# A tuned attention and two-layer MoE kernel: the second layer's sort in two parts, fifteen tiles in the first layer's slot 17 and twelve at the seam

## The chip, the core and the metric

The kernel runs on one core of one Trainium2 chip. A core has five engines with queues of their own: TensorE (PE in the rows; PEld is its weight load), VectorE (DVE), ScalarE (ACT), GpSimd (POOL) and SyncE (SP, which here issues most DMA transfers). Each engine takes its instructions in the order in which the program gives them to it; between engines semaphores hold an instruction back until what it needs is there. The metric is device microseconds (us) for one execution.

## The reference, cut to what matters

Attention over 4 batches of 576 tokens makes x of 2304 rows and 512 columns (not touched here). Two mixture-of-experts layers follow, each with eight experts and one expert for each token:

```python
def _moe2_ref(x, modality_id, w_gate, modality_bias, w1, w2) -> np.ndarray:
    ...
    logits = x @ w_gate + modality_bias[modality_id]
    e_idx = np.argmax(logits, axis=1)
    ...
    gate_w = probs[np.arange(N), e_idx]
    ...
    for e in range(E):
        mask = e_idx == e
        ...
        h = np.maximum(x[mask] @ w1[e], 0.0)
        out[mask] = gate_w[mask, None] * (h @ w2[e])
```

`probs` is the softmax of the logits. The first layer is the same but for a second gate in place of the modality's bias.

## The kernel before, in words

**Slots.** A layer (`moe`, L789 on) works through slots. A slot is one tile of up to 128 tokens that go to the same expert, padded where an expert's last tile isn't full. Slots 0 to 17 always run; slots 18 to 26 stand in nested `tc.If` blocks and run while the number of slots, found at run time, is larger. In slot `s`, `slot()` issues 96 matmuls `ph<-xT,wb` (L834) in two halves of 48, `mm1(0)` and `mm1(1)`; after each half ScalarE makes `hh` (L844) and VectorE `hl` (L845); then 24 matmuls `py<-wb,hh` and `py<-wb,hl` (L905) make the result, 16 with hh and 8 with hl. The two first slots of a layer take their tokens from `xsA` and go to the expert that most tokens want (`first_expert`, `first_slots`, made during the end of the stage before, from part of the tokens); their result stays in `pya0` and `pya1` until the gates are known.

**Weights.** When the expert changes, SP loads 4 MB of f32 weights into `raw` in eight pieces (L89), and ScalarE and VectorE split them into high and low f16 halves `wb` (L97, L102). In slots `s` from 3 on this is done piece by piece inside branches that ask at run time whether the slot after next needs it (`part`, L859). The second layer's slots 0 to 2 use one expert whose weights were loaded and split during the first layer (`Fill`); slot 3 (`KE`) always turns to new weights, and which expert these are stands in the table `tab`.

**Results of the first layer.** In slot `s`, `post.out(s - 1)` takes the previous slot's result out of PSUM: ScalarE writes its high half (L1036), VectorE its low half (L1037). `post.turn(s - 1)` lets TensorE transpose the row of halves behind `mm1(1)` (L1055, eight transposes, the first four on the high half, the last four on the low half), VectorE copies that into `yT` (L1056), TensorE makes the second layer's logits from it (`router`, L1064) and VectorE adds them into `lg2` (L1073). In slot 17 the router runs twice, so that `lg2` is complete up to tile 16 at its end.

**The sort.** `sort()` (L609) is a generator. Between its `yield`s stand the steps that turn logits into slots. Step one classifies: VectorE takes the maximum over eight experts (L620), finds which expert it is (L623 to L632) and counts along the tiles (L635). Step two is TensorE's rank matmuls `ct` and `rk` (L639 to L642). Step three makes positions: VectorE from `cmp` (L646) to the slot and row of each token, `pi` (L675), and the slot matrix `ob` (L679), from which GpSimd makes `obt` (L680) and ScalarE `obp` (L681). Step four lays out rows: `A` is a matrix of 128 columns for each tile with a one in the token's row, made in pieces of nine tiles (L686). Step five is the index matmuls `pidx`, two for each tile (L691, L692). Step six writes `idx` (L696) and issues three gathers of rows from `y_dram` on GpSimd (L797). Step seven, the table, is a chain of VectorE operations from L704 to L732 that ends in `tab`; then TensorE turns slot 2's gathered rows (L812), and SP loads slot 3's weights and transposes its rows. Step eight makes the gates, step nine sums them (`pg`, L772, L774).

**What sets the order.** Nothing is scheduled automatically. `at(s, k, f)` hangs a function at hook `k` of slot `s`: hook 0 is at the slot's start, 8 behind the first eight matmuls, 1 and 4 inside the first and second half (two thirds through), 2 behind the first half and ahead of its hh and hl, 3 behind them, 5 behind the second half's hh and hl and the previous row's transposes, 6 behind 12 of the 24 `py` matmuls, 7 at the slot's end. Before the change the second layer's sort hung wholly in the second layer:

```python
at(0, 8, lambda: post1.router(None), run(so2))
at(0, 6, run(so2))
at(0, 7, run(so2, 2))
at(1, 6, run(so2, 2))
at(1, 7, run(so2))
at(2, 0, run(so2))
```

The seam is the stretch from the first layer's last slot to the second layer's slot 3. With this input the first layer runs 23 slots: slot 17 lies at about 365 to 378 us of the trace, slot 18 starts at 378.23, and the second layer's slot 0 starts its matmuls at 437.42.

## Time and profile before

| | |
|---|---|
| median of 3 runs | 660.2 us (659.15 to 666.1) |
| the profiled execution, its own time | 661.31 us |
| its span in the trace | 659.5 us, mean granted clock 0.953 |
| busy: PE, PEld, DVE, ACT, POOL | 591.5, 459.4, 358.2, 268.9, 204.9 us |

All times in rows are microseconds from the span's start. A row of the timeline has the start, the length of the merged group, the engine, the line, the operation with output and input, how many were merged (x96) and, in brackets, how long the engine had been idle before and what it was released by. A row of the view by stretch has the stretch, its length, the busy time of PE, PEld, DVE, ACT and POOL with the number of instructions in brackets, then TensorE's granted clock as a share of full speed, the busy share of the DMA engines and GB/s. Releasers are inferred: where the engine named had long been done, it was something else, often a DMA.

### The profile page before, as it was taken

What the parts mean: (1) busy time and instruction counts of PE and PEld (TensorE: products, weight loads), DVE (VectorE), ACT (ScalarE), POOL (GpSimd) and SP (SyncE); (2) the same over time, 40 slices, a digit from 0 to 9 for tenths busy, and PEclk for the clock granted to TensorE, in tenths of its full rate; (3) what the DMA queues carried; (4) which work ended last, traced back from release to release, by engine and by line L of the source; (5) the groups of instructions that cost most, each with busy time, mean ns of one, the idle gap of its engine ahead of it and who ended that gap; (6) DMA issues with size and microseconds to landing.
All of it is one profiled execution on the core that took longest, in us unless ns stands there. A gap on an engine that the chain in (4) does not pass through costs nothing. (4 is left out here: it accounts for less than half of the span.)

```text
span 659.5 us, 19565 instructions
## 1 busy us (share of the span) xinstructions
PE 591.5 (90%) x7440; PEld 459.4 (70%) x7440; DVE 358.2 (54%) x656; ACT 268.9 (41%) x398; POOL 204.9 (31%) x327
## 2 busy tenths in 40 slices
PE   3889978942998999999999999989889999999994
PEld 2778877842786776868687686866667767676772
DVE  4699987867848625963848922248351010113560
ACT  4678766642245324833627511111242111123450
POOL 2467677615351111101102410002463312121220
PEclk9789999975798999999999999989899999999997
DMA  9999999997399964995878871500995434243921
GB/s 205 230 233 229 243 223 249 254 271 211 86 330 317 341 162 104 345 321 136 232 222 213 228 141 49 59 28 2 238 357 144 106 89 84 65 97 83 309 57 42
DMA packets 108514, 120.99 MB, mean 183 GB/s; under 512 B 72047, under 2 KB 76911, under 8 KB 107376
## 3 DMA queue, kind: packets, MB, share of 16 engines
q1 hardware_dynamic: 102720, 101.71, 61.7%
q0 software_dynamic: 5280, 17.13, 8.4%
q8 instruction: 60, 0.98, 0.7%
q10 hardware_dynamic: 400, 0.72, 0.5%
q14 instruction: 54, 0.44, 0.2%
HBM read 214.11 MB, written 18.22 MB: 352 GB/s over the span
## 5 line engine op out<-in xcount | busy, mean ns | idle before, releaser
L834 PEld LDWEIGHTS <-wb 128*128 128x128 f16 x4032 | 234.2, 100 | 10.3 <-issue 5.1
L834 PE MATMUL ph<-xT,wb 128*128 128x128 f16 x3648 | 213.5, 221 | 2.8 <-ACT y L1036 1.1
L845 DVE SCALAR_TENSOR_TENSOR hl<-ph,hh 128x512 f16<-128x512 f32 x84 | 57.8, 689 | 169.5 <-ACTq L859 152.0
L905 PE MATMUL py<-wb,hh 128*128 128x512 f16 x608 | 137.6, 379 | 1.6 <-ACTq L859 1.6
L905 PEld LDWEIGHTS <-hh 128*128 128x128 f16 x672 | 63.8, 98 | 70.4 <-ACTq L859 1.7
L102 DVE SCALAR_TENSOR_TENSOR wb<-raw,wb 128x1024 f16<-128x1024 f32 (+1 forms) x80 | 102.9, 1326 | 18.1 <-ACT wb L97 17.9
L844 ACT ACTIVATE hh<-ph 128x512 f16<-128x512 f32 x84 | 50.1, 597 | 147.5 <-PE ph L834 147.0
L97 ACT ACTIVATE wb<-raw 128x1024 f16<-128x1024 f32 (+1 forms) x80 | 86.9, 1133 | 12.0 <-ACTq L859 3.1
L905 PE MATMUL py<-wb,hl 128*128 128x512 f16 x304 | 71.9, 379 | 0.0
L905 PEld LDWEIGHTS <-hl 128*128 128x128 f16 x336 | 32.8, 98 | 39.9 <-DVE hl L845 0.4
L1160 POOL DMA_INDIRECT out<-y,idx x16 | 16.2, 1010 | 97.9 <-ACTq L859 77.7
L421 PE MATMUL po<-v,pT 128*96 128x65 f32 x384 | 39.3, 253 | 1.2 <-DMA v<-in_vw 1.2
L421 PEld LDWEIGHTS po<-v,pT 128*96 128x96 f32 x384 | 36.1, 169 | 1.6 <-DMA v<-in_vw 1.5
L797 POOL DMA_INDIRECT xg<-x_dram,idxaa x23 | 26.7, 1161 | 28.1 <-DMA xT<-xg 17.3
L407 PE MATMUL pst<-mt,msel 128*128 128x96 bf16 x192 | 30.6, 219 | 2.3 <-ACT mt L395 2.2
L362 DVE TENSOR_REDUCE M<-ps 96x4 f32<-96x512 f32 x48 | 31.5, 679 | 2.0 <-PE ps L361 1.9
L1159 ACT ACTIVATE y<-py,gsb 128x512 f32<-128x512 f32 x16 | 11.0, 686 | 52.3 <-PE py L905 52.3
L319 DVE SCALAR_TENSOR_TENSOR kl<-qk,kh 128x608 f16<-128x608 f32 x32 | 28.5, 892 | 7.0 <-ACT kh L316 7.0
L360 PEld LDWEIGHTS <-qs 128*96 128x96 f16 x192 | 24.5, 132 | 11.2 <-DVE qs L341 6.2
L360 PE MATMUL ps<-kh,qs 128*96 128x128 f16 x192 | 29.5, 232 | 2.8 <-ACT kh L316 2.8
L410 ACT ACTIVATE pT<-pst 128x384 f32<-128x384 f32 x48 | 23.4, 488 | 19.3 <-PE pst L409 18.7
L361 PE MATMUL ps<-kl,qs 128*96 128x128 f16 x192 | 29.3, 232 | 1.8 <-DVE kl L319 1.8
(401 smaller groups left out, 750.2 us busy)
## 6 DMA issues: line engine op xcount, KB each, us to landing
raw<-in_w1a SPq DMA_DIRECT2D x95, 512.0 KB
raw<-in_w2a SPq DMA_DIRECT2D x92, 512.0 KB
raw<-in_w1b SPq DMA_DIRECT2D x75, 512.0 KB
raw<-in_w2b SPq DMA_DIRECT2D x72, 512.0 KB
qk<-in_qk SPq DMA_DIRECT2D x16, 608.0 KB
v<-in_vw SPq DMA_DIRECT2D x16, 390.0 KB
qk<-in_qk SPq DMA_DIRECT2D x16, 304.0 KB
y_dram<-y SPq DMA_DIRECT2D x11, 260.0 KB
```

The costliest lines, as they stand in the source:

```text
L97: nc.scalar.activation(wb[:, 0, s], raw[:, s], AF.Copy, scale=SW)
L102: nc.vector.scalar_tensor_tensor(out=wb[:, 1, s], in0=raw[:, s], scalar=SW, in1=wb[:, 0, s], op0=ALU.mult, op1=ALU.subtract)
L319: nc.vector.scalar_tensor_tensor(out=kls[n][:, h], in0=krs[n][:, h], scalar=SQK, in1=khs[n][:, h], op0=ALU.mult, op1=ALU.subtract)
L360: nc.tensor.matmul(ps[:, j, :], st, kh[:, h, QT * i:QT * i + 128], start=False, stop=False, skip_group_check=True)
L361: nc.tensor.matmul(ps[:, j, :], st, kl[:, h, QT * i:QT * i + 128], start=False, stop=j == 3, skip_group_check=True)
L362: nc.vector.tensor_reduce(out=Ms[n][:, 4 * g:4 * g + 4], in_=ps, axis=AX.X, op=ALU.max)
L407: nc.tensor.matmul(ps[:, j, :], msel[:, typ, j, :], mt[:, g, :], start=j == 0, stop=False, skip_group_check=True)
L421: nc.tensor.matmul(po[:, i, :], pT[:, NQ * h + i, :], v[:, h, i, :], start=True, stop=True)
L834: nc.tensor.matmul(ph[:, j, :], w[:, c, fs], xT[:, parts[c + i], :], start=k == 0, stop=k == 47, skip_group_check=True)
L844: nc.scalar.activation(hs, ph, AF.Relu)
L845: nc.vector.scalar_tensor_tensor(out=hl[:, 4 * g:4 * g + 4, :], in0=ph, scalar=0.0, in1=hs, op0=ALU.max, op1=ALU.subtract)
L905: nc.tensor.matmul(to, a, w, start=k == 0, stop=k == len(ops) - 1)
```

## The change

The sort of the second layer becomes two parts. The first fifteen of its 27 tiles (`PRE`) are classified at hook 5 of the first layer's slot 17, ranked among themselves, and given their rows within their expert and the part of `A` for them at hook 7 of that slot; these numbers don't depend on how many blocks each expert gets, only the slot does. At the seam only twelve tiles are classified and ranked, the first part's counts being added by one more matmul to `ct` and one to `rk`; positions are made for all tiles, `A` for the last twelve. The hooks at the seam move too: the rank matmuls from hook 6 of slot 0 to hook 4, the index matmuls and gathers from hook 6 of slot 1 to hook 2, the table from hook 7 to 6, the gates from hook 0 of slot 2 to hook 7 of slot 1, the gates' sums and the first splits of new weights to earlier hooks of slot 2. `oh` and `inc` are now laid out part by part.

```diff
+PRE = 15
...
-    for n in (NT, NSLOT):
+    for n in (NT, PRE, NSLOT - PRE):
...
+        def classify(a, b):
+            n = b - a
+            sh = [P, n, E]
+            v.tensor_reduce(out=mx[:, a:b], in_=lg[:, a:b], axis=AX.X, op=ALU.max)
+            v.tensor_tensor(eq[:, a:b], lg[:, a:b], mx[:, a:b].unsqueeze(2).to_broadcast(sh), op=ALU.is_equal)
+            v.tensor_tensor(eq[:, a:b], eq[:, a:b], desc.unsqueeze(1).to_broadcast(sh), op=ALU.mult)
+            v.tensor_reduce(out=mi[:, a:b], in_=eq[:, a:b], axis=AX.X, op=ALU.max)
+            if inv is not None:
+                v.scalar_tensor_tensor(out=mi[:, a:b], in0=inv[:, a:b], scalar=16.0, in1=mi[:, a:b], op0=ALU.mult, op1=ALU.add)
+            c = min(max(ca, a), b)
+            own = mi
+            if a < c:
+                own = mb
+                v.scalar_tensor_tensor(out=mb[:, a:c], in0=ea["cons"][:, a:c], scalar=16.0, in1=mi[:, a:c], op0=ALU.mult, op1=ALU.add)
+                if c < b:
+                    v.tensor_copy(mb[:, c:b], mi[:, c:b])
+            v.tensor_tensor(part(ohs, a, b).rearrange("p e t -> p t e"), eq[:, a:b], own[:, a:b].unsqueeze(2).to_broadcast(sh), op=ALU.is_equal)
+            v.tensor_tensor_scan(incs[:, E * a:E * b], masks[n].rearrange("p e t -> p (e t)"), ohs[:, E * a:E * b], 0.0, op0=ALU.mult, op1=ALU.add)
+
+        def ranks(a, b):
+            rk = pp.tile([P, E, b - a], F32, name="rk", tag="pw")
+            nc.tensor.matmul(rk, lt1, part(ohs, a, b), start=True, stop=False)
+            nc.tensor.matmul(rk, ones, part(incs, a, b), start=False, stop=a == 0)
+            if a:
+                nc.tensor.matmul(rk, ones, part(incs, 0, a)[:, :, a - 1:a].to_broadcast([P, E, b - a]), start=False, stop=True)
+            return rk
+
+        def rows(a, b):
+            for a in range(a, b, ACH):
+                n = min(ACH, b - a)
+                v.tensor_tensor(A[:, a:a + n], iota_row.unsqueeze(1).to_broadcast([P, n, P]),
+                                pi[:, 2, a:a + n].unsqueeze(2).to_broadcast([P, n, P]), op=ALU.is_equal)
+
+        ps_ = T("ps", [E, -1])
+        if pre:
+            classify(0, pre)
+            yield
+            rk = ranks(0, pre)
+            yield
+            within = T("within", [-1])
+            v.tensor_tensor(ps_[:, :, :pre], rk, part(ohs, 0, pre), op=ALU.mult)
+            v.tensor_reduce(out=within[:, :pre], in_=ps_[:, :, :pre].rearrange("p e t -> p t e"), axis=AX.X, op=ALU.add)
+            v.tensor_tensor(within[:, :ca], within[:, :ca], ea["consr"], op=ALU.add)
+            v.tensor_copy(pi[:, 0, :pre], within[:, :pre])
+            v.tensor_scalar(pi[:, 2, :pre], pi[:, 0, :pre], 127, None, op0=ALU.bitwise_and)
+            yield
+            rows(0, pre)
+            yield
+        classify(pre, nt)
         yield
...
+        nc.tensor.matmul(ct, ones, part(incs, pre, nt)[:, :, nt - pre - 1], start=True, stop=not pre)
+        if pre:
+            nc.tensor.matmul(ct, ones, part(incs, 0, pre)[:, :, pre - 1], start=False, stop=True)
+        rk = ranks(pre, nt)
...
-        ps_ = T("ps", [E, -1])
-        v.scalar_tensor_tensor(out=ps_, in0=rk, scalar=float(KA * P), in1=base.unsqueeze(2).to_broadcast([P, E, nt]), op0=ALU.add, op1=ALU.add)
-        v.tensor_tensor(ps_, ps_, oh, op=ALU.mult)
+        if pre:
+            v.scalar_tensor_tensor(out=ps_[:, :, :pre], in0=base.unsqueeze(2).to_broadcast([P, E, pre]), scalar=float(KA * P), in1=part(ohs, 0, pre), op0=ALU.add, op1=ALU.mult)
+        v.scalar_tensor_tensor(out=ps_[:, :, pre:], in0=rk, scalar=float(KA * P), in1=base.unsqueeze(2).to_broadcast([P, E, nt - pre]), op0=ALU.add, op1=ALU.add)
+        v.tensor_tensor(ps_[:, :, pre:], ps_[:, :, pre:], part(ohs, pre, nt), op=ALU.mult)
         pos = T("pos", [-1])
         v.tensor_reduce(out=pos, in_=ps_.rearrange("p e t -> p t e"), axis=AX.X, op=ALU.add)
-        v.tensor_tensor(pos[:, :ca], pos[:, :ca], ea["consr"], op=ALU.add)
-        pi = T("pi", [3, -1], I32)
+        if pre:
+            v.tensor_tensor(pos[:, :pre], pos[:, :pre], within[:, :pre], op=ALU.add)
+        else:
+            v.tensor_tensor(pos[:, :ca], pos[:, :ca], ea["consr"], op=ALU.add)
         if inv is None:
             v.tensor_copy(pi[:, 0], pos)
         else:
             v.scalar_tensor_tensor(out=pi[:, 0], in0=inv, scalar=8192.0, in1=pos, op0=ALU.mult, op1=ALU.add)
         v.tensor_scalar(pi[:, 1], pi[:, 0], 7, None, op0=ALU.logical_shift_right)
-        v.tensor_scalar(pi[:, 2], pi[:, 0], 127, None, op0=ALU.bitwise_and)
+        v.tensor_scalar(pi[:, 2, pre:], pi[:, 0, pre:], 127, None, op0=ALU.bitwise_and)
...
-        A = T("A", [-1, P], F16)
-        for a in range(0, nt, ACH):
-            n = min(ACH, nt - a)
-            v.tensor_tensor(A[:, a:a + n], iota_row.unsqueeze(1).to_broadcast([P, n, P]),
-                            pi[:, 2, a:a + n].unsqueeze(2).to_broadcast([P, n, P]), op=ALU.is_equal)
+        rows(pre, nt)
...
+    def sort2(n=1):
+        def go():
+            if not sorts:
+                sorts.append(sort("b", lg2, NSLOT, start1.inv, fe2, early[1], tabs[1], 1.0, None, [], 1 / (SX2 * SW * SW), start2, PRE))
+            for _ in range(n):
+                next(sorts[0], None)
+        return go
+
+    for s, k in ((15, 0), (15, 7), (16, 0), (16, 3), (16, 5), (16, 7), (17, 0), (17, 7)):
+        at(s, k, slots2)
+    at(17, 5, sort2())
+    at(17, 7, sort2(3))
+    py1 = moe(w1a, w2a, tabs[0], x_dram, (0, 1, 4, 5, 2, 3, 6, 7), post1, start1, wbuf)
...
-    at(0, 8, lambda: post1.router(None), run(so2))
-    at(0, 6, run(so2))
-    at(0, 7, run(so2, 2))
-    at(1, 6, run(so2, 2))
-    at(1, 7, run(so2))
-    at(2, 0, run(so2))
-    at(2, 5, lambda: start2.first_splits(FIRST[0]), lambda: start2.first_splits(FIRST[1]))
-    at(2, 6, run(so2), lambda: start2.first_splits(FIRST[2]), lambda: start2.first_splits(FIRST[3]))
+    at(0, 8, lambda: post1.router(None), sort2())
+    at(0, 4, sort2())
+    at(0, 7, sort2(2))
+    at(1, 2, sort2(2))
+    at(1, 6, sort2())
+    at(1, 7, sort2())
+    at(2, 3, lambda: start2.first_splits(FIRST[0]))
+    at(2, 5, sort2(), *(lambda i=i: start2.first_splits(FIRST[i]) for i in (1, 2)))
+    at(2, 6, lambda: start2.first_splits(FIRST[3]))
```

**Place 1, VectorE from slot 17's last hl to slot 18's first operation.** The rows are VectorE's instructions in program order. `hl` is the second half's low part, `yT` the copy of the transposed row, `wb` the weight splits in their branches, `lg` the logits of tile 16, `lotmp` the low half of slot 17's result. Before:

```order
L845 SCALAR_TENSOR_TENSOR hl<-ph_6832,hh 128x512
L1056 COPY yT_2814<-pyt 128x1024
L859 COMPARE_AND_BRANCH
L102 SCALAR_TENSOR_TENSOR wb_69<-raw,wb_69 128x1024 x3
L859 UNCONDITIONAL_BRANCH x2
L855 TENSOR_LOAD tab_2800
L859 COMPARE_AND_BRANCH
L102 SCALAR_TENSOR_TENSOR wb_2779<-raw,wb_2779 128x1024 x3
L859 UNCONDITIONAL_BRANCH x2
L1073 SCALAR_TENSOR_TENSOR lg_78<-plg,lg_78 128x8
L922 COMPARE_AND_BRANCH
L1037 SCALAR_TENSOR_TENSOR lotmp<-py,gsa,lotmp 128x512
```

And now, first behind the copy of yT (hook 5):

```order
L1096 COPY yT_2817<-pyt 128x1024
L632 TENSOR_REDUCE mxb<-lg_78 128x15
L633 TENSOR_TENSOR eqb<-lg_78,mxb 128x120
L634 TENSOR_TENSOR eqb<-eqb,cft 128x120
L635 TENSOR_REDUCE mib<-eqb 128x15
L637 SCALAR_TENSOR_TENSOR mib<-inva,mib 128x15
L642 SCALAR_TENSOR_TENSOR mbb<-ea_cons_85,mib 128x13
L644 COPY mbb<-mib 128x2
L645 TENSOR_TENSOR ohb<-eqb,mbb 128x15x8
L646 SCALAR_TENSOR_TENSOR incb<-mask_2807,ohb 128x120
L899 COMPARE_AND_BRANCH
L103 SCALAR_TENSOR_TENSOR wb_69<-raw,wb_69 128x1024 x3
```

then, behind both branches, at hook 7:

```order
L1113 SCALAR_TENSOR_TENSOR lg_78<-plg,lg_78 128x8
L669 TENSOR_TENSOR psb<-rk,ohb 128x8x15
L670 TENSOR_REDUCE withinb<-psb 128x15
L671 TENSOR_TENSOR withinb<-withinb,ea_consr_86 128x13
L672 CAST pib<-withinb 128x15
L673 TENSOR_SCALAR pib<-pib 128x15
L659 TENSOR_TENSOR Ab<-c16t,pib 128x1152
L659 TENSOR_TENSOR Ab<-c16t,pib 128x768
L962 COMPARE_AND_BRANCH
L1077 SCALAR_TENSOR_TENSOR lotmp<-py,gsa,lotmp 128x512
```

Nine instructions moved in between yT's copy and the splits, seven between the logits of tile 16 and `lotmp`'s low half (L1037 before, L1077 now).

**Place 2, TensorE in the second layer's slot 1, at the first index matmuls.** `ph` is the first matmul group, `pya` the second one's result, `pidx` the index sums. Before:

```order
L905 LDWEIGHTS hh
L905 MATMUL pya_8831<-wb_2791,hh 128x512
L691 LDWEIGHTS Ab
L691 MATMUL pidx<-obpb,Ab 128x27
L692 LDWEIGHTS Ab
L692 MATMUL pidx<-obtb,Ab 128x27
```

And now:

```order
L874 LDWEIGHTS wb_2791
L874 MATMUL ph_9076<-xsA_82,wb_2791 128x128
L731 LDWEIGHTS Ab
L731 MATMUL pidx<-obpb,Ab 128x27
L732 LDWEIGHTS Ab
L732 MATMUL pidx<-obtb,Ab 128x27
```

The index matmuls stood behind the twelfth matmul of slot 1's second group; they stand now behind the first half of its first group, with the other half behind them.

**Place 3, VectorE in slot 1, from `ob` to the table's chain** (`e2` and `end` are the chain's first two operations). Before:

```order
L679 TENSOR_TENSOR obb<-bmb,pib 128x729
L686 TENSOR_TENSOR Ab<-c16t,pib 128x1152 x3
L845 SCALAR_TENSOR_TENSOR hl<-ph_9053,hh 128x512
L845 SCALAR_TENSOR_TENSOR hl<-ph_9104,hh 128x512
L696 CAST idxbb<-pidx 128x27
L704 TENSOR_TENSOR e2b<-fe_Mib,nbb 128x64
L705 TENSOR_REDUCE endb<-e2b 128x8
```

And now:

```order
L723 TENSOR_TENSOR obb<-bmb,pib 128x729
L659 TENSOR_TENSOR Ab<-c16t,pib 128x1152
L659 TENSOR_TENSOR Ab<-c16t,pib 128x384
L736 CAST idxbb<-pidx 128x27
L885 SCALAR_TENSOR_TENSOR hl<-ph_9076,hh 128x512
L885 SCALAR_TENSOR_TENSOR hl<-ph_9189,hh 128x512
L744 TENSOR_TENSOR e2b<-fe_Mib,nbb 128x64
L745 TENSOR_REDUCE endb<-e2b 128x8
```

The copy of the indices moved ahead of both hl of slot 1; the table's chain stayed behind them.

## Rows read from the trace of the kernel before

**Rows 1.** Busy us by stretch: PE, PEld, DVE, ACT, POOL; then clock, DMA, GB/s

```profile
422.00:432.00 10.00, 10.00 (x136) 7.87 (x135) 2.90 (x5) 1.88 (x3) 0.00 (x0) 1.00 0.44 55
```

**Rows 2.** Timeline, second layer's slots 0 to 2 (start, length, engine, line, operation)

```profile
447.62 0.31 DVE L646 TENSOR_TENSOR cmpb<-ct,cft 128x144 f32<-128x144 f32 x1 [1.30 <-PE ct L639]
...
450.18 5.52 PE L834 MATMUL ph<-xsA,wb 128*128 128x128 f16 x96
...
452.93 2.39 POOL L680 TENSOR_TENSOR obtb<-obb,cft 128x729 f16<-128x729 f16 x1 [2.24 <-DVE obb L679]
...
459.79 0.21 DVE L704 TENSOR_TENSOR e2b<-fe_Mib,nbb 128x64 f32<-128x64 f32 x1
...
463.18 0.18 DVE L729 SCALAR_TENSOR_TENSOR tab<-nxb,swb 128x26 int32<-128x26 f32 x1
...
463.63 0.61 PE L812 MATMUL pxt<-identh,xg 128*128 128x128 f16 x8 [1.38 <-issue]
...
464.42 1.78 SPq L89 DMA_DIRECT2D raw<-in_w1b  x3
...
465.34 7.01 PE L834 MATMUL ph<-xT,wb 128*128 128x128 f16 x96 [1.10 <-ACT xT L813]
```

**Rows 3.** Timeline, slot 3: the last weights, and what waits for them

```profile
483.78 1.91 ACT L97 ACTIVATE wb<-raw 128x2048 f16<-128x2048 f32 x1 [1.63 <-DMA raw<-in_w2b]
...
487.09 3.63 PE L905 MATMUL py<-wb,hh 128*128 128x512 f16 x16 [1.57 <-ACTq L859]
```

**Rows 4.** Timeline, first layer, slot 17's end and slot 18: VectorE and TensorE

```profile
373.73 0.68 DVE L1056 COPY yT<-pyt 128x1024 f16<-128x1024 f16 x1
...
374.33 3.48 DVE L102 SCALAR_TENSOR_TENSOR wb<-raw,wb 128x1024 f16<-128x1024 f32 x3
...
378.40 0.17 DVE L1073 SCALAR_TENSOR_TENSOR lg<-plg,lg 128x8 f32<-128x8 f32 x1 [0.59 <-PE plg L1064]
378.84 0.75 DVE L1037 SCALAR_TENSOR_TENSOR lotmp<-py,gsa,lotmp 128x512 f16<-128x512 f32 x1 [0.27 <-ACTq L859]
...
383.58 0.61 PE L1055 MATMUL pyt<-identh,lotmp 128*128 128x128 f16 x8
```

**Rows 5.** Timeline, VectorE: first and last operation classifying 18, then 27 tiles

```profile
159.79 0.30 DVE L620 TENSOR_REDUCE mxa<-lg 128x18 f32<-128x144 f32 x1
...
162.36 0.46 DVE L635 TENSOR_TENSOR_SCAN inca<-mask,oha 128x144 f16<-128x144 f16 x1
...
439.44 0.38 DVE L620 TENSOR_REDUCE mxb<-lg 128x27 f32<-128x216 f32 x1
...
442.85 0.61 DVE L635 TENSOR_TENSOR_SCAN incb<-mask,ohb 128x216 f16<-128x216 f16 x1
```

**Rows 6.** Timeline, VectorE: rows of five tiles; positions and rows of 27

```profile
359.90 0.81 DVE L252 TENSOR_TENSOR Ac<-c16t,pic 128x640 f16<-128x640 f16 x1
...
450.05 0.41 DVE L665 TENSOR_TENSOR psb<-psb,ohb 128x216 f32<-128x216 f32 x1
...
451.58 0.18 DVE L674 TENSOR_SCALAR pib<-pib 128x27 int32<-128x27 int32 x1
...
452.70 5.10 DVE L686 TENSOR_TENSOR Ab<-c16t,pib 128x1152 f16<-128x1152 f16 x3
```

**Rows 7.** Timeline, TensorE at the seam's start: two waits, the burst behind

```profile
436.40 0.40 PE L1055 MATMUL pyt<-identh,y 128*128 128x128 f16 x4 [1.59 <-ACT y L1032]
...
438.71 6.24 PE L834 MATMUL ph<-xsA,wb 128*128 128x128 f16 x88
```

**Rows 8.** Busy us by stretch, as rows 1, after waits near 464 and 486

```profile
466.00:467.00 1.00, 1.00 (x13) 1.00 (x11) 0.50 (x2) 0.00 (x0) 0.32 (x1) 0.50 0.93 332
...
487.00:488.00 1.00, 0.91 (x5) 0.44 (x6) 1.00 (x1) 0.63 (x2) 1.00 (x1) 1.00 0.99 393
```

**Rows 9.** One line's instructions (ns; first and last start): half the index matmuls

```profile
L692 PE MATMUL pidx<-obtb,Ab x27: 174/175/176, 458.2 to 459.5; 128*128 128x27 f16 x27
```

**Rows 10.** The page, part 5: one group (us, mean ns; idle before)

```profile
L845 DVE SCALAR_TENSOR_TENSOR hl<-ph,hh 128x512 f16<-128x512 f32 x84 | 57.8, 689 | 169.5 <-ACTq L859 152.0
```

## The prediction, as it was recorded before the run

> **What bounds the kernel now.** The busy times by stretch come first. In the first layer's last slots TensorE is busy in every microsecond at full clock, while VectorE works for 2.9 us in ten [rows 1]: what holds TensorE up there is paid in full, and what VectorE does beside it is free until TensorE asks for it. The timeline shows TensorE waiting for microseconds behind slot 17 only around the seam between the layers. In the second layer's first slots there are two waits ahead of slot 2, 1.38 and 1.10 us, and then 96 matmuls that take 7.01 us where they take 5.52 in slot 1 [rows 2]. But slot 3 is set by something else: ScalarE waits 1.63 us for the last weights to land, splits them until 485.69, and TensorE waits 1.57 us for what is queued behind that [rows 3]. These weights are asked for by SP at 464.42, just after VectorE has written the expert table at 463.18 [rows 2]. So the chain through the seam is the table, the transfers, the splits, slot 3. TensorE's waits before slot 2 are slack against it.

> **The pre-part in slot 17.** Sixteen VectorE instructions go into slot 17: nine that classify fifteen tiles, behind the copy of yT and ahead of three weight splits; then five that make positions and two that lay out rows, behind L1073 and ahead of L1037 in slot 18. VectorE takes them in order, and L1037 makes the low half of the row that TensorE transposes at 383.58 [rows 4]. Behind these transposes stands all of slot 18's second matmul group.

> Prices. Classifying 18 tiles took from 159.79 to 162.82, 3.03 us, and 27 tiles from 439.44 to 443.46, 4.02 us [rows 5]; the larger has one small operation more. For fifteen I take 3.0, with bounds 15/27 of 4.02, 2.2, and the whole 4.0. Positions took 1.71 us for 27 tiles in six operations (450.05 to 451.76); here there are five, on fifteen tiles: 1.25, bounds 0.95 and 1.71. Rows took 5.10 us in three pieces of nine tiles, 1.70 a piece, but 0.81 for five tiles elsewhere [rows 6]; a piece of nine and one of six is 2.8 by the first and 2.4 by the second. I take 2.8, since nine is the size used.

> The VectorE queue then reads: copy of yT done at 374.41; classify to 377.4; three splits, 3.48, to 380.9; branches, between 0.27 and 0.59 by the idle times in rows 4, say 0.4, to 381.3; L1073 to 381.5; positions to 382.7; rows to 385.5; a branch, 0.27; L1037, 0.75, to 386.55. Before, TensorE took the low half at about 383.85, halfway through its eight transposes. It now waits **2.7 us**; with all low bounds 1.0, with all high ones 4.3. Two more small matmuls in slot 17 (ranks) lie ahead of that wait and shorten it by as much as they cost. The splits, 3 us later, still end before the second group needs them.

> Such a wait may cost the clock too. At the seam's start waits of 1.59 us and less lie close together, and the 88 matmuls behind take 6.24 us [rows 7] where 88/96 of 5.52 is 5.06: 1.2 lost. [...] After the single wait of 1.57 us near 486 the clock stayed at 1.00 [rows 8]. A wait of 2.7 us is nearer to the pairs that fell: I take **1.5 us**, bounds 0 and 1.5.

> [...]

> **The seam with twelve tiles.** Classifying twelve is about 2.5 us instead of 4.02 (bounds 1.8 and 4.0), and the rank matmuls move from slot 0's second group into its first. VectorE's next work, cmp, waited 1.30 us for them until 447.62, so slot 0's second hl had ended at 446.32 [rows 2]. Now that hl comes 0.4 us later, for five small matmuls ahead of it (eight transposes take 0.61), and cmp starts behind it at 446.75: 0.9 us gained. One operation more and smaller ones balance; so GpSimd's obt, which runs 2.39 us, ends at 454.5 instead of 455.3, and VectorE's rows, 2.3 us instead of 5.10, at 454.1. But the index matmuls now stand behind slot 1's first half of 96, at 450.2 + 2.8 = 453.0. So TensorE **waits there about 1.5 us**, for obt, with 48 matmuls and slot 1's second group queued behind. The gathers then start some 3.7 us earlier than before, and the transposes for slot 2 find their rows: 1.38 and 1.10 us of waiting go. Slot 2 starts about 0.4 us earlier than 465.34.

> What does this do for slot 3? The table chain stands behind slot 1's second hl in VectorE's queue. That hl follows TensorE's second half, which now ends at 453.0 + 1.5 + 1.4 (index matmuls, from 458.1 to 459.5 before [rows 9]) + 2.8 = 458.7; ScalarE's hh and then hl take some 0.7 each (hl's mean is 689 ns [rows 10], hh is as wide), so hl ends near 460.2. Before, the chain started at 459.79. So the table is written **0.4 us later**, not earlier, SP asks for the weights 0.4 us later, and slot 3 follows. The waits freed before slot 2 turn into a longer wait in slot 3. The gathers no longer share the DMA engines with the first weights, which could return something; I keep +0.4, bounds -0.7 and +1.0. The first split and the gate matmuls, now earlier in slot 2, hang on the same landings: nothing.

> **The sum.** 2.7 + 1.5 + 0.4 = 4.6 us: the profiled execution's span would be 664.1 and its own time 665.9 instead of 661.3. The median of the runs shown is 660.2, 1.1 below the profiled time, so **664.8**.

> **Rivals.**
> 1. The wait in slot 18 comes, the clock stays. For it: 1.57 us did not lower it. Then 2.7 + 0.4, 663.3.
> 2. The pre-part is hidden, every piece near its low bound. Against it: between 374 and the transposes VectorE's idle time is the 4.3 us behind L1037, shared with one hl, and I count 3.0 + 1.25 + 2.8 = 7 us. Then only the seam is left: 660.6.
> 3. It ends faster, by one mechanism: slot 3 follows slot 2 and not the weights. The earlier gathers take out 1.38, 1.10 and 1.49 us, and slot 3's 1.57 goes too: 5.5 us, against 4.2 lost in slot 18, 658.9. It decides where the table is written before about 459, 4.2 us ahead of 463.18. The VectorE order, with the chain still behind both hl, speaks against it. [...]
> 4. The new wait at the index matmuls lowers the clock in slot 1: the second half takes 1.5 us longer, and table, weights and slot 3 follow: 666.3.

> **How the numbers follow.** Chances: the forecast 0.50 (its own range 663 to 666), clock unharmed 0.17, hidden 0.10, faster 0.08, the fourth 0.15. The range 660.5 to 667 leaves out the third rival, the low edge of the second and high bounds that meet, together 0.2. One per cent, about what a measurement here can tell from no change, is 6.6 us: below 653.6 no case ends, 0.03; above 666.8 lies the fourth with high bounds, 0.12; within, 0.85.

> **What would show it.** In slot 18 TensorE's transposes of lotmp should wait 2 to 3 us for L1077 (L1037 before), with clock 0.50 in the stretch behind. In slot 1 the first pidx matmul should wait over 1 us for POOL's obt. No wait should stand ahead of slot 2's first matmul, SP's first raw<-in_w1b after the seam should lie no earlier, counted from the seam's start, than before, and slot 3's waits should grow. The forecast is wrong if slot 18 shows no wait, or if the weights are asked for 2 us earlier or more.

## The result, and the profile after

| | before | after |
|---|---|---|
| median of 20 runs each | 662.78 us (658.65 to 668.14) | 666.66 us (663.91 to 669.63) |
| ratio, with its 95% interval | | 1.0054 [1.0031, 1.0077] |
| the profiled execution, its own time | 661.31 us | 666.70 us |
| its span, mean granted clock | 659.5 us, 0.953 | 664.9 us, 0.960 |

The change costs 0.54%, that is 3.6 us (2.1 to 5.1). The forecast was 664.8 us, 4.6 above its base of 660.2; the time fell into its range and on its side of one per cent. That base, a median of three runs, was 2.6 us below the median of twenty, so the time lies near the top of the range. The sum came out near, but half of its terms did not. To see that, the spans alone don't help: they differ by 5.4 us, but 3.6 of these arise before the first of the moved work runs. So the executions are cut at marks of TensorE that every kernel has: the router matmuls `plg` (slot 17's first; those of the first layer's last slot; those in the second layer's slot 0) and slot 3's first `py` matmul. The timeline has them, before:

```profile
364.39 0.45 PE L1064 MATMUL plg<-wr2h,yT 128*128 128x8 f16 x12
...
434.36 0.45 PE L1064 MATMUL plg<-wr2h,yT 128*128 128x8 f16 x12
...
438.37 0.48 PE L1064 MATMUL plg<-wr2h,yT 128*128 128x8 f16 x12 [0.22 <-DVE yT L1056]
```

and after, with slot 3's mark as the last line (before, it is the 487.09 of [rows 3]):

```profile
368.02 0.45 PE L1104 MATMUL plg<-wr2h,yT 128*128 128x8 f16 x12
...
439.42 0.45 PE L1104 MATMUL plg<-wr2h,yT 128*128 128x8 f16 x12
...
445.04 0.48 PE L1104 MATMUL plg<-wr2h,yT 128*128 128x8 f16 x12 [0.31 <-DVE yT L1096]
...
491.88 3.63 PE L945 MATMUL py<-wb,hh 128*128 128x512 f16 x16 [0.33 <-ACTq L899]
```

| stretch | before | after | difference | forecast |
|---|---|---|---|---|
| up to slot 17's mark | 364.39 | 368.02 | +3.63 | 0 |
| **slots**: slot 17's mark to the last slot's | 69.97 | 71.40 | +1.43 | +4.2 |
| **end**: from there to slot 0's mark | 4.01 | 5.62 | +1.61 | 0 |
| **seam**: from there to slot 3's `py` | 48.72 | 46.84 | -1.88 | +0.4 |
| slot 3's `py` to the last slot's | 158.16 | 158.76 | +0.60 | 0 |

The first line is how executions differ: two experiments below whose program is that of before up to slot 17 have 369.95 and 365.82 there. The next three lines are the change: a third of the price foreseen in the slots, a loss at the end of the first layer that no step foresaw, and a gain at the seam. The last line scatters too, from 158.1 to 159.9 in all profiles, and by 1.1 between two profiles of the changed kernel.

**Slots.** VectorE behind slot 17, timeline after:

```profile
377.97 0.27 DVE L632 TENSOR_REDUCE mxb<-lg 128x15 f32<-128x120 f32 x1
...
380.48 0.41 DVE L646 TENSOR_TENSOR_SCAN incb<-mask,ohb 128x120 f16<-128x120 f16 x1
380.81 3.47 DVE L103 SCALAR_TENSOR_TENSOR wb<-raw,wb 128x1024 f16<-128x1024 f32 x3
...
384.50 0.27 DVE L669 TENSOR_TENSOR psb<-rk,ohb 128x120 f32<-128x120 f32 x1
...
385.91 2.23 DVE L659 TENSOR_TENSOR Ab<-c16t,pib 128x1152 f16<-128x1152 f16 x2
388.05 0.75 DVE L1077 SCALAR_TENSOR_TENSOR lotmp<-py,gsa,lotmp 128x512 f16<-128x512 f32 x1
```

TensorE's low-half transposes, and the clock of the stretch behind them:

```profile
388.86 0.40 PE L1095 MATMUL pyt<-identh,lotmp 128*128 128x128 f16 x4 [1.15 <-DVEq L899]
```

```profile
388.00:392.00 4.00, 3.15 (x18) 1.61 (x19) 2.78 (x5) 0.12 (x1) 0.00 (x0) 1.00 0.97 140
```

The order is the forecast one: classify 377.97 to 380.89, positions 384.50 to 385.88, rows, then L1077, which TensorE waits for. It waits 1.15 us, and the clock stays at 1.00. From the start of the first four of these transposes to `py` it takes 1.77 us instead of 0.45, and the two rank matmuls ahead of slot 18 take 0.1: together the stretch's 1.4 us.

**End.** In the last slot before the seam VectorE does nothing for 2.97 us before L1073, with nothing to wait for; TensorE's second four transposes wait 1.99 us for it, 0.39 before:

```profile
441.47 0.40 PE L1095 MATMUL pyt<-identh,y 128*128 128x128 f16 x4 [1.60 <-ACT y L1072]
443.05 0.75 DVE L1073 SCALAR_TENSOR_TENSOR y<-py,prg,y 128x512 f16<-128x512 f32 x1 [2.97 <-issue]
443.86 0.40 PE L1095 MATMUL pyt<-identh,y 128*128 128x128 f16 x4 [1.99 <-DVE y L1073]
```

**Seam.** TensorE, GpSimd, ScalarE and SP, timeline after, to be read against [rows 2, 3]:

```profile
458.23 2.39 POOL L724 TENSOR_TENSOR obtb<-obb,cft 128x729 f16<-128x729 f16 x1 [2.04 <-DVE obb L723]
...
460.67 0.17 PE L732 MATMUL pidx<-obtb,Ab 128*128 128x27 f16 x1 [0.96 <-POOL obtb L724]
...
467.69 1.04 PE L945 MATMUL pya<-wb,hh 128*128 128x512 f16 x4 [1.11 <-ACT hh L884]
...
471.60 5.52 PE L874 MATMUL ph<-xT,wb 128*128 128x128 f16 x96
...
472.79 2.43 SPq L90 DMA_DIRECT2D raw<-in_w1b  x3
...
479.80 1.21 PE L814 MATMUL pg<-Bgb,Ab 128*128 128x81 f16 x27 [2.00 <-POOL Bgb L807]
...
488.56 1.91 ACT L98 ACTIVATE wb<-raw 128x2048 f16<-128x2048 f32 x1 [0.79 <-DMA raw<-in_w2b]
```

Slot 2's matmuls start without a wait and at a granted clock of 1.00 (5.52 us instead of 7.01). In exchange there are three waits: 0.96 at the index matmuls, 1.11 for `hh`, 2.00 for the gates' `Bgb`. Counted from slot 0's mark, the weights are asked for 27.75 us later, 26.05 before: 1.7 later, and still slot 3 comes 1.9 earlier. What shrank is the way from the request to the last split's start: 464.42 to 483.78 before, 19.4 us; 472.79 to 488.56 after, 15.8.

### The profile page after: what moved, and what is told of

Read it like the earlier page. It is cut to its first block, busy times and chain, and to the rows that moved or that the text cites. A ratio compares the mean times of both kernels' runs of the same rounds, so it can differ in the third digit from the quotient of the medians.

```text
span 664.9 us, 19587 instructions
## 1 busy us (share of the span) xinstructions
PE 588.6 (89%) x7444; PEld 455.6 (69%) x7444; DVE 361.3 (54%) x670; ACT 269.3 (41%) x398; POOL 203.0 (31%) x329
## 5 line engine op out<-in xcount | busy, mean ns | idle before, releaser
L874 PEld LDWEIGHTS <-wb 128*128 128x128 f16 x4032 | 231.4, 99 | 8.5 <-issue 3.7
L1194 ACT ACTIVATE y<-py,gsb 128x512 f32<-128x512 f32 x16 | 11.0, 686 | 51.6 <-PE py L945 48.7
L411 ACT ACTIVATE pT<-pst 128x384 f32<-128x384 f32 x48 | 23.4, 489 | 18.0 <-PE pst L410 17.1
L408 PE MATMUL pst<-mt,msel 128*128 128x96 bf16 x192 | 28.9, 213 | 1.6 <-ACT mt L396 1.6
```

Source lines behind the costliest of these rows:

```text
L408: nc.tensor.matmul(ps[:, j, :], msel[:, typ, j, :], mt[:, g, :], start=j == 0, stop=False, skip_group_check=True)
L874: nc.tensor.matmul(ph[:, j, :], w[:, c, fs], xT[:, parts[c + i], :], start=k == 0, stop=k == 47, skip_group_check=True)
```

## The experiments

The theory by then: rows in slot 17 make the wait there; L1073 is late because of where VectorE's program lies in instruction memory; the seam gains from transfers that come faster. The rivals: the clock; something in the data path ahead of L1073; an earlier slot 2. Ratios are against runs of the kernel before on the same chip; the three columns of stretches come from each profile.

| run | ratio [95%] | slots | end | seam | sum against before |
|---|---|---|---|---|---|
| before | | 69.97 | 4.01 | 48.72 | |
| after | 1.0054 [1.0031, 1.0077] | 71.40 | 5.62 | 46.84 | +1.2 |
| e1_pre_alone | 1.0061 [1.0030, 1.0092] | 71.79 | 5.88 | 48.42 | +3.4 |
| e2_seam_alone | 1.0000 [0.9965, 1.0035] | 69.98 | 4.02 | 50.01 | +1.3 |
| e3_moved_code | 1.0074 [1.0039, 1.0110] | 73.65 | 4.01 | 46.82 | +1.8 |
| e4_after_again | 1.0041 [1.0012, 1.0070] | 71.41 | 5.62 | 46.99 | +1.3 |
| e5_code_alone | 1.0047 [1.0021, 1.0073] | 71.41 | 6.67 | 47.18 | +2.6 |
| e6_rows_at_seam | 1.0026 [0.9992, 1.0059] | 70.17 | 6.45 | 45.50 | -0.6 |
| e7_table_early | 1.0025 [0.9998, 1.0051] | 71.64 | 6.72 | 44.02 | -0.3 |
| e8_all_three | 0.9990 [0.9963, 1.0018] | 70.14 | 6.49 | 42.48 | -3.6 |
| e9_all_code_moved | 0.9990 [0.9964, 1.0016] | 70.09 | 4.02 | 41.82 | -6.8 |
| e10_after_code_moved | 1.0096 [1.0059, 1.0134] | 71.42 | 4.01 | 46.93 | -0.3 |
| e11_whole_early | 0.9965 [0.9939, 0.9991] | 69.98 | 4.01 | 46.01 | -2.7 |
| e12_all_code_in_slots | 0.9964 [0.9937, 0.9992] | 70.44 | 4.02 | 43.01 | -5.2 |

### The two halves of the change apart

e1 keeps slot 17's part and gives the seam its hooks of before; e2 has before's whole sort with the new hooks.

```diff
 e1, against after
-    at(0, 4, sort2())
+    at(0, 6, sort2())
-    at(1, 2, sort2(2))
-    at(1, 6, sort2())
-    at(1, 7, sort2())
+    at(1, 6, sort2(2))
+    at(1, 7, sort2())
+    at(2, 0, sort2())
...
 e2, against before
-    at(0, 6, run(so2))
+    at(0, 4, run(so2))
-    at(1, 6, run(so2, 2))
-    at(1, 7, run(so2))
-    at(2, 0, run(so2))
+    at(1, 2, run(so2, 2))
+    at(1, 6, run(so2))
+    at(1, 7, run(so2))
...
```

> The changed kernel's work in slot 17 (15 tiles classified, ranked and laid out), but every step of the sort at the seam where the kernel before has it. Three theories. (A) Slots 17 and 18 cost what the changed kernel's trace shows, a wait of TensorE of 1.1 us and rank matmuls of 0.4, so the last router matmuls of the first layer move by +1.4 us against the first half of slot 17; and VectorE's late start at the seam (2.97 us idle, TensorE waits 2.0 us instead of 0.39) comes from the 18 instructions that now stand ahead of it, so it is here too: +1.6. The seam itself returns to about what it was, since gathers and table stand at the same places: sum +3.0, ratio 1.0045. (B) The late start belongs to something else, it is not here: sum +1.4, ratio 1.002. (C) What the pair of traces showed ahead of slot 17 (+3.6 us) is the change's own doing: ratio 1.007 or more, and the first half of slot 17 starts 3 us later than in the trace of the kernel before.

> The kernel before with the changed kernel's places at the seam and the sort whole there: 27 tiles classified, ranks in the middle of slot 0's second half, the index matmuls in slot 1 after its first half, the first splits in slot 2 one place earlier. Nothing in slot 17. (A) The index matmuls wait for the rows of all 27 tiles, 5.1 us on VectorE after ob instead of 3.0 for 12: a wait of about 3 us at pidx instead of 1.0, gathers about 2 us later than in the changed kernel, the table 2 us later; slot 3 loses the 1.9 us that the seam of the changed kernel gained: within 0.5 us of the kernel before, ratio 0.999 to 1.001. Slot 18 shows no wait for L1037, and VectorE starts at the seam as before. (B) The gain lies in the places alone (gathers ahead of the weights' transfers): seam -1.9 us, ratio 0.997. (C) The wait at pidx is paid in full: +2 us, ratio 1.003.

e1 has the slots' and the end's loss whole and almost nothing of the seam's gain (48.42). e2 has neither loss, and its seam is slower than before's, 50.01: without the part in slot 17 the earlier index matmuls wait for `obt` and twice for rows of `A`, and 48 matmuls behind them take 4.45 us, at a granted clock of 0.50 from 464 to 466 us, where 2.84 at 1.00 is what after shows. Timeline of e2, TensorE in slot 1:

```profile
459.64 0.17 PE L692 MATMUL pidx<-obtb,Ab 128*128 128x27 f16 x1 [1.05 <-POOL obtb L680]
...
460.85 0.19 PE L691 MATMUL pidx<-obpb,Ab 128*128 128x27 f16 x1 [0.64 <-DVE Ab L686]
...
462.12 0.19 PE L691 MATMUL pidx<-obpb,Ab 128*128 128x27 f16 x1 [0.65 <-DVE Ab L686]
```

So at these hooks the two halves need each other: the shorter sort opens the place that the earlier hooks use, and each alone gains 0.3 or loses 1.3 at the seam where both gain 1.9. At other hooks they don't, as e11 shows below.

### Where VectorE's code lies

The trace's branch and semaphore records show VectorE's 2.97 us more closely. Behind L1113 it leaves the last run slot's block, lands behind the blocks of slots that did not run, handles two semaphores, branches once more and then stands still:

```
VectorE, us                                  before     after
compare-and-branch, leaves the block         434.861    439.920
first semaphore record where it lands        435.381    440.442
compare-and-branch there                     435.595    440.655
next semaphore record, ahead of L1033/L1073  435.794    442.861
L1033 / L1073 starts                         436.382    443.047
```

Between the second compare-and-branch and the semaphore record behind it lie 0.20 us before and 2.21 after. Instruction transfers appear around this moment. The view of the DMA queues from the last slot's mark on, 434.36 to 441.00 before and 439.42 to 446.06 after, has two packets before and three after, of 8,192 bytes each; the third starts at 443.46, 0.6 us behind the end of the stall:

```profile
q14 instruction: 2, 0.02, 0.6%
```

```profile
q14 instruction: 3, 0.02, 1.2%
```

To move only the code, one-element memsets were put into VectorE's program of the changed kernel: ahead of it and in slots 7 to 15 (e3), into a slot that is never run (e5), only ahead of it (e10).

```diff
 e3 (55), e10 (32), at the program's start
+        for _ in range(32):
+            nc.vector.memset(mbr[0][0:1, 0, QT:QT + 1], 0.0)
...
 e3, in five slots
+    for s in (7, 9, 11, 13, 15):
+        at(s, 4, pad)     # 11 memsets
...
 e5, in slot 26, which doesn't run
+    at(26, 7, pad)        # 110 memsets
```

> The changed kernel with 110 writes of one element more on VectorE (0.06 us each): 55 at the start, where it waits for the first inputs, and 11 each in slots 7, 9, 11, 13 and 15. With the 18 instructions of the change VectorE's code at the seam then lies 128 instructions, 8 KB, behind where the kernel before has it. (A) The late start at the seam comes from where that code lies in the blocks of 8 KB in which instructions are fetched: it goes away, VectorE's y L1073 follows ScalarE's y L1072 at once, TensorE waits 0.4 us there instead of 2.0, and the time is 1.6 us below the changed kernel's, less what the writes cost (some 0 to 1 us): ratio to the kernel before 1.003. (B) It comes from anything else (a semaphore, the branches of the slots not run): VectorE stays idle about 3 us, ratio 1.0054 or a little more.

> The changed kernel once more, for a second trace of it. (A) The 3.6 us ahead of slot 17 are how executions differ: the first half of slot 17 starts somewhere between 365 and 369 us, VectorE is idle 3 us at the seam again, TensorE waits 1.1 us in slot 18 and again 2.0 us at the seam. (B) They are systematic: slot 17 starts at 369 or later again. Ratio 1.0054 within 0.003 under both.

> The changed kernel with 110 writes of one element more on VectorE, all of them in the last slot of the first layer, which this input does not run: VectorE's code at the seam lies 128 instructions behind where the kernel before has it, and nothing is executed for that. (A) VectorE's late start goes away as it did with the writes spread over the program: TensorE waits 0.4 us for y L1073 at the seam, not 2.0; from the last router matmuls of the first layer to those at the seam 4.0 us instead of 5.6. Slots 17 and 18 still cost +1.4, the seam still gives back 1.8: in all -1.6 against the changed kernel, about 0 against the kernel before: ratio 0.998 to 1.003. (B) What matters is the code that lies ahead of the jump, which is now longer: VectorE stays late, ratio 1.004 to 1.006.

> The changed kernel with 32 writes of one element on VectorE at the start and nothing else. (A) As above: no stall at the seam, 4.0 us between the last router matmuls of the first layer and those at the seam, against 5.6 in the changed kernel; slots 17 and 18 +1.4, slot 3 at 46.9 (-1.8): in all -0.4 by the stages, and a ratio 1.6 us below the changed kernel's: 0.999 to 1.003. (B) 5.6 us again, ratio 1.004 to 1.006. (C) The stages come out so but the ratio stays over 1.004: something ahead of slot 17 costs time that a single trace does not show.

e4, the changed kernel again, repeats each of the three stretches within 0.15 us. e3 takes the end's loss away whole (4.01) but has a loss of its own in slot 17, where TensorE waits 1.74 us (1.13 in after) for logits that VectorE adds, and needs 4.47 us (2.84 in after) for the 48 matmuls behind, at a granted clock of 0.50 from 376 to 378 us. e5, which runs not one instruction more, makes the end worse: 6.67. Now ScalarE waits too, for a semaphore of VectorE's queue, and TensorE behind it:

```profile
445.08 0.69 ACT L1072 ACTIVATE y<-py,prg 128x512 f16<-128x512 f32 x1 [8.59 <-DVEq L962]
...
445.83 0.61 PE L1095 MATMUL pyt<-identh,y 128*128 128x128 f16 x4 [4.05 <-ACT y L1072]
```

e10 takes the loss away with 32 memsets that run at the start, and VectorE's start is released by the data again:

```profile
445.64 0.75 DVE L1075 SCALAR_TENSOR_TENSOR y<-py,prg,y 128x512 f16<-128x512 f32 x1 [1.37 <-ACT y L1074]
...
446.45 0.40 PE L1097 MATMUL pyt<-identh,y 128*128 128x128 f16 x4 [0.39 <-DVE y L1075]
```

The time as a whole does not fall with it: e10's ratio, 1.0096, is the highest of all, and the last part of this section comes back to that.

Counted in instructions from the start of VectorE's program, semaphores and branches included:

| kernel | leaves at | lands at | `y`'s semaphore at | stall |
|---|---|---|---|---|
| before, e2, e11 | 1264 | 1388 | 1406 | none |
| after, e1, e4 | 1282 | 1406 | 1424 | 2.2 us ahead of `y` |
| e5 to e8 | 1280 or 1282 | 1516 | 1534 | 3.07 us at the jump (e5), 0.52 in the other lines |
| e3 | 1392 | 1516 | 1534 | none |
| e9, e10 | 1314 | 1438 | 1456 | none |
| e12 | 1316 | 1440 | 1458 | none |

### The rows, and the table

e6 leaves classes and positions in slot 17 and lays out the fifteen tiles' rows at the seam. e7 moves the index matmuls into slot 1's second half, two thirds through it, with the table chain and slot 3's first weights right behind, ahead of the second hl. e8 does both. All three carry e5's unused code, so e5 is what to hold them against.

```diff
 e6
...
-            rows(0, pre)
-            yield
         classify(pre, nt)
...
         rk = ranks(pre, nt)
+        if pre:
+            rows(0, pre)
...
 e7
...
-    at(1, 2, sort2(2))
+    at(1, 4, sort2(3))     # index matmuls, gathers, table, first weights
     at(1, 6, sort2())      # gates
     at(1, 7, sort2())      # slot 2's rows turned, the other weights
```

> As the run before, and the rows of the 15 tiles are laid out at the seam, with the ranks in slot 0 of the second layer, instead of in slot 17 (2.2 us of VectorE; there it waits 2.1 us for ScalarE's hh). (A) They are what TensorE waits for in slot 18: its 1.15 us go, and of +1.4 some 0.4 for the rank matmuls are left; at the seam cmp starts 0.1 to 0.5 us later. Ratio 0.997 to 1.001, 1 us below the run before. (B) L1077 is late for the positions or the splits ahead of them: the wait in slot 18 stays over 0.7 us.

> The changed kernel with the same 110 writes in the slot that is not run, and at the seam the index matmuls in the middle of slot 1's second half instead of ahead of it; directly behind them indices, gathers and the table chain, on VectorE ahead of slot 1's second hl; the weights' first transfers follow the table; gates at the end of slot 1, then TensorE's turning of the first tile. (A) The index matmuls find obt done (its 1.0 us wait goes), ScalarE's hh in slot 1 comes at once (1.1 us goes), the table stands some 5 us earlier, the gates with it, so the wait for Bgb (2.0 us) in slot 2 goes: slot 3's second half starts up to 4 us earlier, counted from the seam's router matmuls (46.8 us in the changed kernel, 48.7 in the one before): 43 to 44.5. Ratio 0.992 to 0.996. (B) The weights' transfers meet the gathers again, as in the kernel before, and slot 3 waits for them: 46 to 48 us, ratio 0.998 to 1.003. (C) The second hl is late behind the table chain and TensorE waits in slot 1 for 1 us or more: 45 to 46.5.

> The rows at the seam and the early table together, with VectorE's code 128 instructions behind. (A) The gains add: slot 18 without its wait (-1.1), slot 3's second half at 43.5 to 45 us from the seam's router matmuls. Ratio 0.990 to 0.995, faster than both kernels. (B) The rows in slot 0 push cmp, ob and with them the index matmuls back, so that these wait again: what slot 18 gives, slot 1 takes, ratio as in the run before.

e6 brings the slots back to 70.17: L1077 is in time, and the low half is transposed with no wait.

```profile
380.99 0.75 DVE L1077 SCALAR_TENSOR_TENSOR lotmp<-py,gsa,lotmp 128x512 f16<-128x512 f32 x1
```

```profile
382.36 0.61 PE L1095 MATMUL pyt<-identh,lotmp 128*128 128x128 f16 x8
```

The rows were the whole wait. Laid out at the seam they cost nothing there: the index matmuls wait 0.95 us, 0.94 in e5, and the seam is 45.50 against e5's 47.18, mostly because the weights come faster after the request (16.2 us to the last split's start, 18.3 in e5), for which the edit gives no reason. e7 shortens the seam by 3.2 against e5: no wait at the index matmuls, for `hh` or for `Bgb`; the one left is 1.10 us for slot 2's rows. The 44.02 of the seam is what was expected; the ratio, not told apart from 1, isn't. e8 has both gains. Its seam is 6.2 shorter than before's, but the end's 2.5 us and about 2 us that the next section comes back to eat most of that: its ratio, expected at 0.990 to 0.995, is not told apart from 1.

### Versions meant to be faster

e9 is e8 with the code moved by 34 memsets at the start instead of the unused ones, e12 the same by nine memsets each in slots 7, 9, 11 and 13. e11 is the kernel before, its sort whole, with e7's hooks alone.

```diff
 e11, against before
-    at(0, 6, run(so2))
+    at(0, 4, run(so2))
-    at(1, 6, run(so2, 2))
-    at(1, 7, run(so2))
-    at(2, 0, run(so2))
+    at(1, 4, run(so2, 3))
+    at(1, 6, run(so2))
+    at(1, 7, run(so2))
...
```

> The rows at the seam and the early table together, as two runs before, but instead of the writes in the slot that is not run, 34 writes of one element on VectorE at the start, where it waits for its first inputs; nothing else is added. Jump and target at the seam then both lie 32 instructions further than in the changed kernel. (A) VectorE stalls when the jump out of the last slot that runs, the block of semaphores it lands in, or the code behind it stands in a block of 8 KB beyond the next one: in the changed kernel jump, landing and code stand at 1282, 1406 and 1424 of VectorE's instructions, and the third crosses into one more block; with the writes in the slot that is not run 1282, 1516 and 1534, the second crosses. Here 1314, 1438 and 1456 stand in two blocks that follow each other: no stall, 4.0 us from the last router matmuls to those at the seam instead of 6.5. With slot 3's second half at 42.5 us from there, as in the run with the writes in the last slot, the sum is 6.1 us below the kernel before: ratio 0.991, 0.988 to 0.995. (B) Only a shift by whole blocks helps: 5.6 us or more again, ratio 0.995.

> The kernel before, its sort whole at the seam and nothing in slot 17, with the places of the early table: ranks in the middle of slot 0's second half, index matmuls, gathers and table chain in the middle of slot 1's, gates at its end, first splits in slot 2 one place earlier. (A) The rows of 27 tiles are 2.1 us longer on VectorE than those of 12 and the classifying 1 us: the index matmuls wait some 2 us for them, and slot 3's second half starts at 44 to 45 us from the seam's router matmuls (42.5 with the sort in two parts, 48.7 before); slots 17 and 18 as in the kernel before, the seam starts after 4.0 us: ratio 0.993 to 0.995. Then most of what can be had here lies in the places, and the sort in two parts adds 2 us. (B) The wait grows over 3 us and the clock falls behind it, as where the hooks alone were moved: 46 to 48 us, ratio 0.997 to 1.000; then it is the sort in two parts that makes the early places worth anything.

> The rows at the seam and the early table together, with 36 writes of one element on VectorE in the first layer's slots 7, 9, 11 and 13, nine in each, where it waits for ScalarE, and none at the start of the program. (A) The seam is as with the writes at the start: 4.0 us from the last router matmuls to those at the seam, slot 3's second half 42 us from there, by the stages 6.5 us below the kernel before; and what the two kernels with the writes at the start lost ahead of the first layer's slots (their times were 6 us above what their stages say) does not come back, since nothing is changed there: ratio 0.990 to 0.994. (B) The loss ahead of the slots has nothing to do with the writes at the start: the stages again say -6.5 us, and the ratio is 0.997 to 1.001.

All three have the end of before, 4.01 or 4.02, but none reaches its expected ratio: 0.9990 for 0.988 to 0.995, 0.9965 for 0.993 to 0.995, 0.9964 for 0.990 to 0.994. e11 is faster than the kernel before, 0.9965, with no part of this change's split: a median of 660.16 us against 662.95. Its table is begun at 459.20, ahead of slot 1's second hl, and slot 2 starts behind a single wait; the seam, 46.0, still ends one us later than expected, since the index matmuls wait for rows of `A` and slot 3's `py` waits 1.34. Timeline of e11:

```profile
458.44 0.19 PE L691 MATMUL pidx<-obpb,Ab 128*128 128x27 f16 x1 [0.65 <-DVE Ab L686]
...
459.20 0.21 DVE L704 TENSOR_TENSOR e2b<-fe_Mib,nbb 128x64 f32<-128x64 f32 x1
...
463.96 1.77 SPq L89 DMA_DIRECT2D raw<-in_w1b  x3
...
466.69 5.52 PE L846 MATMUL ph<-xT,wb 128*128 128x128 f16 x96 [1.10 <-ACT xT L825]
```

e12 comes to the same ratio, 0.9964, though its stretches sum to 2.5 us less than e11's. So the split in two parts, repaired of all that it cost, is worth nothing that these runs can tell beside the order of the hooks.

**What stays open.** The ratios give more than the stretches. For the eight runs with the split sort and no memsets at the start (after, e1, e4 to e8, e12) the timed difference is 0.5 to 2.9 us above the stretches' sum, 1.9 on the mean; with memsets at the start, which lie ahead of the first mark (e3, e9, e10), 3.1 to 6.7; for the two with the whole sort (e2, e11) -1.3 and +0.4. A single interval is some 1.5 to 2.5 us wide on each side, so no run shows it alone, but the signs agree. The stretch behind slot 3 accounts for part (158.1 to 159.9 in all profiles); the stretch up to slot 17, which scatters from 361 to 372 in single profiles, could hold the rest. It is 371.1 on the mean of the three profiles with memsets at the start and 366.5 on that of the other eleven, but e5 and e7, whose programs are the same up to there, lie 8.8 apart, so single profiles don't settle it. So e10 has the stall gone from its stretch and no gain in its time; that the kernel as a whole becomes faster without the stall is not shown.

## Why the prediction was right, point by point

**Slot 17's pre-part: the mechanism right, the size too large.** TensorE waits for L1077 as the prediction said, 1.15 us instead of 2.7 and just above the low bound. Classifying fifteen tiles took 2.92 (forecast 3.0), positions 1.38 (1.25). The step that failed is the rows: 2.23 instead of 2.8. Nine tiles were priced at 1.70, the mean of the three pieces in [rows 6]. By the view of that line's instructions, before, this mean mixes two kinds:

```profile
L686 DVE TENSOR_TENSOR Ab<-c16t,pib x3: 1346/1351/2558, 452.7 to 456.5; 128x1152 f16<-128x1152 f16 x3
```

Two pieces of 1.35 and one of 2.56, the one that runs beside GpSimd's `obt` of 2.39 us ([rows 2]). After, it is the piece of three tiles that meets `obt`, timeline after:

```profile
459.27 1.76 DVE L659 TENSOR_TENSOR Ab<-c16t,pib 128x384 f16<-128x384 f16 x1
```

Three tiles with nothing beside them took 0.54 us before (L252, at 361.83). Both pieces last until `obt` is done and then 1.21 and 0.41 us more, a little less than their own length. In the first layer's sort, before, `obt` takes 2.05 us and the piece of nine that meets it 2.15, with its end again 1.21 us behind. In slot 17, where `obt` does not run, nine tiles took 1.36 us and six 0.95.

The wait is 1.55 us shorter than forecast. Rows account for 0.65 of it from start to start, the branches for 0.6 (put at 0.4 and 0.27, they show 0.1 ahead of L1113 and nothing ahead of L1077), and TensorE asks 0.2 later, half of it for the rank matmuls; classify and positions about cancel.

**The clock: not lowered.** The term of 1.5 us, what [rows 2] show lost behind two waits (7.01 us for 5.52) at the 0.50 of [rows 8], was rival 1's question, and rival 1's mechanism is what came: the wait of 1.15 is shorter than the 1.57 of [rows 8] that left the clock alone. That a single wait can be followed by a lower clock shows in e3: behind 1.74 us in slot 17 stand 48 matmuls in 4.47 us at a granted clock of 0.50.

**The end: not foreseen, +1.6.** The prediction has no term for the code between the slots and the seam, where no instruction is changed. What it did not look at is where that code lies: eighteen instructions more ahead of it, semaphores counted, put its last step 18 further on (1424 for 1406), and there it stalls.

**The seam: five steps, two right.** The index matmuls wait for `obt` (0.96, forecast 1.5), and slot 2's first half starts 0.4 us earlier from slot 0's mark (26.56 against 26.97), as said. The table is later by 1.8 us, not 0.4: slot 1's second `hh` comes 2.1 us late for a reason that the last section leaves open, and the table's chain stands behind its hl. e5, where this `hh` is in time, has the weights asked for 25.5 us after slot 0's mark, half a microsecond ahead of before's 26.05: without that accident the forecast's step was near. "The gate matmuls, now earlier in slot 2, hang on the same landings: nothing" failed: they stand in TensorE's queue ahead of slot 2's second group and wait 2.00 us for `Bgb`.

And "slot 3 follows" the weights failed in its size: the weights, asked for 1.7 us later, were split 3.6 us sooner after the request. The term was named ("could return something") with a bound of -0.7; it was mis-sized by about 3. So the seam came out at -1.9, outside the bounds of -0.7 and +1.0, and slot 3's wait shrank where the prediction had it grow. Across the runs:

| last gather issued | request to last split's start, us |
|---|---|
| 1.5 to 1.8 us ahead of the weights | before 19.4, e1 18.7, e7 17.1, e8 17.3, e9 17.0, e11 18.6, e12 18.2 |
| 5.3 us ahead | e5 18.3, e6 16.2 |
| 7.4 to 7.5 us ahead | after 15.8, e2 17.3, e3 15.4, e4 16.0, e10 15.8 |

The first and last lines' means are 18.0 and 16.1, which speaks for the gathers. e5 speaks against them as the whole cause: it asks 2.2 us sooner than after, counted from slot 0's mark, and its last split starts 0.3 later. Other transfers moved too and no run changed the gathers alone, so this stays open.

**Rival 3's mechanism came, without its gain.** Slot 3 waits only 0.33 us for what is queued behind the last split (1.57 in [rows 3]) and otherwise follows slot 2, which was that rival's mechanism. Its decider, a table before 459, was wrong: the table was later. Its price, a gain of 5.5, was not reached because the waits moved into slots 1 and 2; e7 and e9, with the table early, reach 4.7 and 6.9 at the seam.

**Rival 2 did not come, rival 4 not as it was put.** The pre-part is not hidden, and behind the 0.96 us at the index matmuls the second half of slot 1 is recorded at a granted clock of 1.00, 2.84 us for 48. That a lowered clock there was possible shows in e2, where three waits make it 4.45. What rival 4 expected of it came nevertheless, a late `hh` and with it a late table and late weights; the last section has what is known of that.

**The sum.** 4.6 forecast, 3.6 timed. In its place stand +1.4, +1.6, -1.9, about +0.6 behind slot 3, and some 2 us that no stretch shows. The stretches that the prediction summed up to +4.6 show +1.2. That the time came near all the same, through a stall that it did not see, the scatter behind slot 3 and some 2 us that stay unexplained, is luck; the number was better than its working.

## What to carry to other kernels

Read the single instructions of a group before its mean is used as a price: one piece held up beside another engine (2.56 us, the other two 1.35) makes the mean wrong for all. Work moved ahead of a wait gained 0.3 us here while the hooks behind it stayed (e1), and when they moved as well the next thing in each queue had to be priced too (the gates, 2 us); moving the order alone, with nothing split, was the better change. Code added ahead of a jump cost 1.6 us at the jump here (after), and code added between a jump and where it lands, not run at all, 2.7 (e5): an idle stretch that ends in "issue" right behind a branch is to be compared in a variant with the code shifted.

## What the runs showed of the hardware that was not expected

- A stall of VectorE behind a jump, 2.2 us (after) where 0.20 is usual or 3.07 us (e5) where 0.52 is, which appears and disappears with the position of its program alone, with one instruction packet of 8,192 bytes more behind it (three instead of two).
- A VectorE operation on rows that starts while GpSimd's `obt` runs beside the piece ahead of it is held until `obt` is done: it ends 1.21 us behind `obt` with an own length of 1.35 us (before, in both layers' sorts), 0.41 behind with 0.54 (after).
- In slot 1 after, `hh` starts at 467.04, though TensorE's last matmul record of that half starts near 464.65; the semaphore that releases it is recorded at 467.02. e3, e4 and e10 show the same. It is gone where the index matmuls stand inside the half (e7 to e9, e11, e12), but in e5 and e6 too, where they stand as in after: there `hh` starts 2.9 us behind the half's first matmul, and here 5.0. In e2, whose matmuls are recorded at a lowered clock, it is 5.0 as well; here the granted clock is 1.00 from 462 to 467. Timeline after, ScalarE:

```profile
467.04 0.60 ACT L884 ACTIVATE hh<-ph 128x512 f16<-128x512 f32 x1 [3.94 <-remote]
```

What holds that semaphore for over 2 us is open; it is 1.1 us of TensorE's time in slot 1, and it makes the table late.
